# Seven products instead of eight for half of the first product in blocks 4 and 5, with their weight sums made in block 0, and 84 products of block 0 made as column halves

## The chip, the cores and the metric

The kernel runs on one core of one Trainium2 chip. A core has a matrix engine (TensorE, PE in the profile; its weight loads are the row PEld), a vector engine (VectorE, DVE), a scalar engine (ScalarE, ACT), GpSimd (POOL) and a queue processor that issues DMAs (SyncE, SP). Each engine works through its own instructions in order and waits for the others through semaphores. The metric is the device time of one execution in microseconds (us), lower is better; the kernel before takes 196.34 us, the median of three runs (196.23 to 196.53).

## The reference

Two parts, one behind the other. A recurrent attention without softmax over 4 batches, 8 heads, 768 steps, heads of 64:

```python
for t in range(S):
    state = gamma * state + outer(k[t], v[t])       # per batch and head, 64 x 64
    y[t] = scale * (q[t] @ state)
x = y, as 3072 tokens x 512
h = x @ w_in                                        # 512 -> 2048
g = h * tanh(softplus(h))                           # "mish"
out = g @ w_out                                     # 2048 -> 512, float32
```

The recurrence is computed in chunks of 128 steps (scores inside a chunk, a state between chunks), so nearly all of the work is matrix products: of the attention, the first product (x with W_in), and the second product (g with W_out).

## The kernel before, in words

The 24 chunks of 128 tokens are taken in 11 blocks. Block 0 has four chunks (512 tokens), blocks 1 to 10 have two (256 tokens). Operands are float16, sums are float32 in PSUM. For each block TensorE makes the first product, ScalarE applies mish, TensorE makes the second product, and between the products of the second one TensorE makes the attention of the block after (`retain`: past states, present scores, and with `later` also the scores and outer products of the block after that one). All instructions are written in the order that each engine runs them; there is no scheduler.

**The second product** of blocks 1 to 10 (`seven`, matrix products at L838) is cut into 2x2 parts and made with seven products of parts instead of eight (Winograd's form of Strassen's scheme). It needs sums of parts of g (`sums_a`, `sums_b`, `sums_c`: DVE, L699, L700, L704, L708, tile gsum) and of W_out (tmat, L683 to L686, made once in block 0). ScalarE copies partial results out (snap, L844), DVE adds them up into osb (`done`, L853 and L851), and SP stores osb (L226).

**The first product** has two forms.

- Plain (`g1`, L635), blocks 0 to 5: for each of 16 groups of 128 features, four matrix products over the 512 inputs; 64 instructions of 256 columns per block (block 0: of 512 columns), and eight mish (L643) of 128x512.
- Mixed (`mixed_in`), from block `MIX` = 6 on: half of the features (quarters 0 and 2 of W_in) by seven products of parts, 56 instructions of 128 columns (L745), the other half plain, 32 instructions of 256 columns (L765). The seven products need sums of W_in (`in_sums`, wsum, L716 to L719, made one operation at a time in blocks 4 and 5) and of x: `x_sums` (L732, four operations of 128x256 float16, two float16 tiles of SBUF in, one out), which DVE makes at the end of the second product of the block before. Results are put together from ScalarE copies (`kept`, L775) and DVE additions (`plus`, L780, tile hsum), then mish (L756).

In a mixed block the order on TensorE is: pa (8 products), a plain pair of groups (8), pf (8, needs the first x sum), a plain pair (8), pm, pa, pf (8 each), a plain pair (8), pa (8), a plain pair into the bank ph (8), pa (8). The bank ph is one that the scores of the block after have held: it comes free when DVE has made the mask product am (`mask_two`, L540) of them. The last pa products add onto a bank that DVE's third addition (h22) must have read. In the code:

```python
        h22 = plus(pa, m5)
        ...
        ph = atps.tile([P, 2, 2, 2 * C], FP32, name="h_ps", tag="at")[:, 0]
        plain(ph, 3 * n + 2)()
        mm(pa, a(1, 1), t[3])
```

On DVE, around the start of a mixed block, stand in this order: an osb sum, x sums 1 and 2, an osb sum, an osb copy, x sums 3 and 4, then the state of the block after (mid, sth, mid: L505 or L507, L516, L507), its mask am, and the three additions h11, h12, h22.

**GpSimd** casts and scales what the loads bring: for each chunk q (L414), k (L417) and v (L424), reading float32 and writing float16 in SBUF, 128x512 each. Where these casts stand is set by `cast_behind` (called in `seven`), which first copies one element of a gsum tile (tile summed, L1179) so that the casts come after that DVE sum, and by what `hooks` puts behind the attention: `next_two` up to block 4 (casts of two chunks), `next_one` from block 5 on. With `next_one` goes `second_of`, called at the start of blocks 6 and later: it first copies one element of the last x sum (L1161), then casts. Each cast pair is turned by a DMA transpose (L429) that SP issues.

**Block 0** loads the weights. Its first two feature groups are made by `open_in` (L620), the other 14 by `g1` (56 instructions of 512 columns), the second product by `g2_mm` without the seven-product scheme (64 instructions of 512 columns, L649). A table `plan` in `first_block` puts other work between its 32 steps: step 9, 12 and 16 cast quarters of W_out on DVE (L220), step 17 starts the W_out sums.

Of the kernel before, what the change touches and what calls it, by code (L numbers as in the profile page):

```python
# [16 lines left out]
def kernel(  # L17
# [9 lines left out]
    nc = tc.nc  # L27
    B, H, S, D = q.shape
    d_model, d_ff = moe_w_in.shape
    P = 128  # L30
# [8 lines left out]
    NFB = d_ff // P  # L39
# [79 lines left out]
    loaded, cast, qkts, ats, ams, states, mids, us, ys = {}, {}, {}, {}, {}, {}, {}, {}, {}  # L119
    xts, gts, wins, wouts, wtmps = {}, {}, {}, {}, {}  # L120
    gtiles, tmats, gsums = {}, [], []
    ONE, MIX = 3, 6
    nload, ncast = [0], [0]
    stores, weight_left, wsums = [], [], []

# [502 lines left out]
    def g1(blk, u):  # L628
        nt = BLOCKS[blk] * C
        per = TB // nt  # L630
        h_ps = g1_bank(blk, u)
        for j in range(per):
            s, f = divmod(u * per + j, FPS)
            for bp in range(NBP):
                nc.tensor.matmul(  # L635
                    h_ps[:, j], wins[s][f // 2][:, bp, f % 2 * P:(f % 2 + 1) * P], xts[blk][:, bp, :nt],
                    start=(bp == 0), stop=(bp == NBP - 1))
        room = NFB * TB // (2 * nt)
        at0, lies = divmod(u * per, room)
        if lies == 0:  # L640
            gtiles[blk, at0] = gp.tile([P, room, nt], FP16, name="g", tag="g", bufs=3)
        gt = gtiles[blk, at0][:, lies:lies + per]
        nc.scalar.activation(gt, h_ps, AF.Mish, scale=inv_boost3)  # L643
        for j in range(per):
            gts[blk, u * per + j] = gt[:, j]

    def g2_mm(o_ps, blk, t, fb, cols=slice(None)):
        s, f = divmod(fb, FPS)
        nc.tensor.matmul(  # L649
            o_ps, gts[blk, fb][:, t * P:(t + 1) * P], wouts[s][:, f, cols],  # L650
            start=(fb == 0), stop=(fb == NFB - 1))

    def out_rows(blk, t):
        if blk == 0:
# [306 lines left out]
    def first_block():  # L961
# [93 lines left out]
        def sum_weights(half, n):  # L1055
            if not weight_left:
                weight_left.extend(weight_sums(half))
            for _ in range(n):
                weight_left.pop(0)()

        plan = {
            9: [(cast_wout, 0)],
            12: [(cast_wout, 1)],
            16: [(cast_wout, 2), (load_more,), (cast_qk,)],
            17: [(sum_weights, 0, 3)],
            23: [(cast_wout, 3, True)],
# [91 lines left out]
    def second_of(blk):  # L1158
        g = first[blk] + 6
        if g < NCK:  # L1160
            nc.gpsimd.tensor_copy(summed, xts[blk + 1][:, 3, TB - 1:])  # L1161
            casts_qk(g + 1)
            turn_by_dma(g + 1)
            casts_v(g)
            casts_v(g + 1)
        store_due(NFB)
        load_to(g + 4)
# [8 lines left out]
    def cast_behind(blk, i):  # L1176
        g = first[blk] + (6 if blk == 1 else 8)
        if ncast[0] < min(g, NCK):
            nc.gpsimd.tensor_copy(summed, gsums[blk % 2][:, i, NFB // 2 - 1, P - 1:])  # L1179
            if blk == 1:  # L1180
                for n in range(g - 2, g):
                    casts_qk(n)
                for n in range(g - 2, g):
                    casts_v(n)
                ncast[0] = g
            elif blk + 1 >= MIX:
                cast_to(g - 2)
                casts_qk(g - 2)
                ncast[0] = g
            else:  # L1190
                cast_to(min(g, nload[0]))
# [5 lines left out]
    def plan_of(blk):  # L1197
        a = first[blk] + 4
        plan = {u: [] for u in (0, 1, 5)}
        if tight(blk):  # L1200
            plan[5] = [(get_ready, blk + 1)]
        elif blk < MIX:
            plan[0] = [(settle, blk + 1), (mask_two, blk + 1), (leave, blk + 1)]
        if blk == 1:
            plan[0] += [(load_to, a + 2)]
            plan[1] += [(begin_load, a + 2)]
        elif blk < ONE:
            plan[1] += [(next_chunk, a)]
        return plan

    first_block()
    for blk in range(1, len(BLOCKS)):
        last = blk + 1 == len(BLOCKS)
        plan = plan_of(blk)
        if blk >= MIX:
            second_of(blk - 1)
            mixed_in(blk, last)
        elif blk > ONE:
            weight_left.extend(in_sums(blk - ONE - 1))
        for u in range(NFB // 2 if blk < MIX else 0):  # L1220
            store_due(u)
            g1(blk, u)
            if u in ((6, 7) if tight(blk) else (5, 7)):
                sums_a(blk, u // 7)
            for fn, *args in plan.get(u, ()):
                fn(*args)
            if weight_left:
                weight_left.pop(0)()
        hooks = [[], [], []]
        if not last:  # L1230
            later = blk + 2 if ONE <= blk < len(BLOCKS) - 2 else None
            hooks = [[(retain, blk + 1, later)],
                     [(next_one, first[blk] + 6)] if blk + 1 >= MIX else
                     [(next_two, first[blk] + 6, tight(blk))] if blk >= ONE else
                     [(turn_load, first[blk] + 4)] if blk == 1 else
                     [(next_chunk, first[blk] + 5), (turn_load, first[blk] + 6)],
                     [(finish, blk + 1)] if later is None else []]
        if tight(blk):
            hooks[2].append((leave, blk + 1))
        seven(blk, [(mask_two, blk + 1)] if tight(blk) else [], hooks, last)  # L1240
# [31 lines left out]
```

## Time and profile before

| what | value |
|---|---|
| median of three runs | 196.34 us (196.23 to 196.53) |
| the profiled execution's own time | 196.27 us |
| its span, first to last instruction | 194.5 us |
| granted TensorE clock | 0.998 of full |
| busy: PE, DVE, ACT, POOL | 189.6, 128.7, 99.5, 73.3 us |
| block 4, plain: first product, whole block | 6.99, 14.45 us |
| block 5, plain: first product, whole block | 6.99, 14.44 us |
| block 6, mixed: first product, whole block | 6.69, 14.21 us |
| block 7, mixed: first product, whole block | 6.69, 14.04 us |

The rows on blocks come from the chain of work that ended last, by the start of each block's first product (93.75, 108.20, 122.64, 136.85 and 150.89 us). In a row of a timeline the first number is the start in us from the begin of the span, the second the duration, then engine, line of the kernel, operation and tiles; in square brackets is the idle time before it and what ended it. The work outside the span (196.27 less 194.5) is 1.8 us.

### The profile page before, as it was taken

How to read it: one execution, taken by the hardware profiler on the slowest of the kernel's cores; microseconds unless marked ns; L12 is line 12 of the kernel's file. 1: busy time of each engine (PE TensorE's matmuls, PEld its weight loads, DVE VectorE, ACT ScalarE, POOL GpSimd, SP SyncE). 2: the span in 40 equal slices, each digit the busy share in tenths (PEclk: the TensorE clock that was granted, in tenths of full speed). 3: DMA queues.
4: the chain of work that ended last, by engine and by line, in shares of the span. 5: the costliest groups of instructions: out<-in, count | busy, mean ns of one | idle time of the engine just before them, and what ended most of it. 6: DMA issues, size and time to landing. Idle time of an engine off the chain costs nothing.

```text
span 194.5 us, 6886 instructions
## 1 busy us (share of the span) xinstructions
PE 189.6 (97%) x2996; PEld 154.0 (79%) x2996; DVE 128.7 (66%) x248; ACT 99.5 (51%) x183; POOL 73.3 (38%) x96
## 2 busy tenths in 40 slices
PE   7998999999999999999999999999999999999994
PEld 7756444454888888888888888998998998988983
DVE  0796535889767378467884864965885885876462
ACT  3375764243553552554364364584574663763750
POOL 5262000549508746562826605525625700000000
PEclk9999999999999999999999999999999999999999
DMA  5999999999999999999999999889996250300202
GB/s 172 304 309 349 368 386 366 293 302 202 202 260 248 157 233 225 214 175 216 261 207 227 278 192 287 103 225 245 77 223 123 50 150 5 111 0 20 95 27 81
DMA packets 84285, 38.75 MB, mean 199 GB/s; under 512 B 57760, under 2 KB 78880, under 8 KB 84256
## 3 DMA queue, kind: packets, MB, share of 16 engines
q1 hardware_dynamic: 84112, 38.28, 84.7%
q8 instruction: 23, 0.38, 0.9%
q10 hardware_dynamic: 144, 0.05, 0.1%
q14 instruction: 6, 0.05, 0.1%
HBM read 27.31 MB, written 6.29 MB: 173 GB/s over the span
## 4 chain that ended last, share of the span: by engine, by line
PE 93%; DMA 3%; ACT 1%; DVE 1%; issue 1%; SPq 0%
PE o_ps L838 32%; PE h_ps L635 24%; PE h_ps L765 9%; PE h_ps L745 8%; PE o_ps L649 7%; PE y_ps L551 3%; DMA qfirst<-in_q_dram 3%; PE u_ps L479 1%; PE at L472 1%; PE t_ps L247 1%; PE y_ps L373 1%; PE h_ps L620 1%; PE at L443 1%; PE at L327 1%; DVE qk L259 1%
## 5 line engine op out<-in xcount | busy, mean ns | idle before, releaser
L635 PE MATMUL h_ps<-xt,win 128*128 128x256 f16 (+1 forms) x376 | 48.5, 289 | 0.0
L635 PEld LDWEIGHTS <-win 128*128 128x128 f16 x376 | 36.5, 98 | 10.4 <-issue 0.2
L643 ACT ACTIVATE g<-h_ps 128x512 f16<-128x512 f32 x54 | 32.2, 597 | 23.7 <-PE h_ps L635 23.7
L838 PEld LDWEIGHTS <-gsum 128*128 128x128 f16 x320 | 30.3, 98 | 3.8
L838 PE MATMUL o_ps<-tmat,gsum 128*128 128x256 f16 x240 | 29.8, 273 | 0.0
L838 PEld LDWEIGHTS <-g 128*128 128x128 f16 x248 | 23.4, 98 | 2.7
L853 DVE TENSOR_TENSOR osb<-o_ps,snap 128x256 f32<-128x256 f32 (+1 forms) x33 | 13.8, 418 | 14.0 <-PE o_ps L838 8.9
L844 ACT COPY snap<-o_ps 128x256 f32<-128x256 f32 (+1 forms) x33 | 12.2, 370 | 20.7 <-PE o_ps L838 20.7
L414 POOL TENSOR_TENSOR qk<-qf,qvs 128x512 f16<-128x512 f32 x18 | 19.2, 1065 | 4.8 <-DMA qf<-in_q_dram 4.7
L765 PE MATMUL h_ps<-xt,win 128*128 128x256 f16 x160 | 20.7, 273 | 0.0
L424 POOL TENSOR_TENSOR v<-vf,qvs 128x512 f16<-128x512 f32 x18 | 19.7, 1101 | 1.2 <-DMA vf<-in_v_dram 1.0
L417 POOL TENSOR_TENSOR qk<-kf,qvs 128x512 f16<-128x512 f32 x18 | 19.1, 1060 | 2.7 <-DMA kf<-in_k_dram 2.6
L838 PE MATMUL o_ps<-wout,g 128*128 128x256 f16 x160 | 19.1, 273 | 0.0
L1179 POOL COPY summed<-gsum 128x1 f16<-128x1 f16 x7 | 3.0, 432 | 37.2 <-DVE gsum L704 29.8
L765 PEld LDWEIGHTS <-win 128*128 128x128 f16 x160 | 14.8, 98 | 1.4
L756 ACT ACTIVATE g<-h_ps 128x512 f16<-128x512 f32 x25 | 14.2, 588 | 2.4 <-PE h_ps L765 2.4
L600 ACT CAST xt<-y_ps 128x512 f16<-128x512 f32 x15 | 10.2, 734 | 10.2 <-PE y_ps L551 10.2
L649 PE MATMUL o_ps<-wout,g 128*128 128x512 f16 x64 | 15.0, 380 | 0.0
L780 DVE TENSOR_TENSOR hsum<-h_ps,hsum 128x512 f32<-128x512 f32 x15 | 10.4, 692 | 6.1 <-PE h_ps L745 4.4
L775 ACT COPY hsum<-h_ps 128x512 f32<-128x512 f32 x15 | 8.8, 585 | 10.5 <-PE h_ps L745 10.5
L699 DVE TENSOR_TENSOR gsum<-g 128x512 f16<-128x512 f16 x20 | 9.2, 459 | 5.2 <-ACT g L643 3.1
L507 DVE TENSOR_TENSOR mid<-u_ps,sth 128x256 f16<-128x256 f32 x15 | 6.3, 422 | 8.5 <-PE u_ps L479 8.2
(99 smaller groups left out, 277.7 us busy)
## 6 DMA issues: line engine op xcount, KB each, us to landing
kf<-in_k_dram SPq DMA_DIRECT2D x24, 256.0 KB, 5.3
vf<-in_v_dram SPq DMA_DIRECT2D x24, 256.0 KB, 5.5
out_dram<-osb SPq DMA_DIRECT2D x22, 256.0 KB, 3.5
qf<-in_q_dram SPq DMA_DIRECT2D x20, 256.0 KB, 4.3
wi<-in_moe_w_in_dram SPq DMA_DIRECT2D x6, 512.0 KB, 8.7
wt<-in_moe_w_out_dram SPq DMA_DIRECT2D x3, 1024.0 KB, 10.3
qfirst<-in_q_dram SPq DMA_DIRECT2D x2, 512.0 KB, 4.6
wi<-in_moe_w_in_dram SPq DMA_DIRECT2D x1, 1024.0 KB, 10.0
```

The lines of the kernel that those rows point to most:

```text
L414: nc.gpsimd.tensor_tensor(in_place(q16.rearrange("p (w x) d -> p w x d", x=2)), by_head(qf), scale_by_head(qs_two[:, heads]), op=ALU.mult)
L417: nc.gpsimd.tensor_tensor(k16.rearrange("p (y w) d -> p w y d", y=2), kf.rearrange("p (w y) d -> p w y d", y=2), boosts.rearrange("p (w y) ...
L424: nc.gpsimd.tensor_tensor(cast[g][2], loaded.pop(g)[2], vs[g % 2].unsqueeze(2).broadcast_to((P, H, D)), op=ALU.mult)
L635: nc.tensor.matmul(h_ps[:, j], wins[s][f // 2][:, bp, f % 2 * P:(f % 2 + 1) * P], xts[blk][:, bp, :nt], start=(bp == 0), stop=(bp == NBP - 1))
L643: nc.scalar.activation(gt, h_ps, AF.Mish, scale=inv_boost3)
L649: nc.tensor.matmul(o_ps, gts[blk, fb][:, t * P:(t + 1) * P], wouts[s][:, f, cols], start=(fb == 0), stop=(fb == NFB - 1))
L745: nc.tensor.matmul(o_ps[:, f], w(f // 2, k)[:, f % 2 * P:(f % 2 + 1) * P], x[:, k], start=begin and f == 0 and k == 0, stop=k == 1, skip_g ...
L756: nc.scalar.activation(to, src, AF.Mish, scale=inv_boost3)
L765: nc.tensor.matmul(h_ps[:, f], wins[w][h // 2][:, k, h % 2 * P:(h % 2 + 1) * P], xts[blk][:, k, :2 * C], start=k == 0, stop=k == NBP - 1)
L838: nc.tensor.matmul(o_ps[:, cols], x(f), w(f)[:, cols], start=first and z == 0, stop=z == n - 1, skip_group_check=True)
L844: nc.scalar.copy(x, o_ps[:, cols])
L853: nc.vector.tensor_tensor(dst, o_ps[:, cols], plus, op=ALU.add)
```

## The change

Three things are changed.

- `MIX` goes from 6 to 4: blocks 4 and 5 take the mixed form. What the old number also decided about casts and loads (`next_one`, `second_of`, the form of `cast_behind`) now goes by a new number `BACK`, which stays at 6: GpSimd's and SP's instructions stand in the same order as before.
- The sums of W_in (two sets of four operations) are made in block 0, at steps 10 and 13, instead of in blocks 4 and 5.
- In block 0 the last 24 instructions of the first product (feature groups 10 to 15) and 60 of the second (all but the first feature group) are each made as two instructions of 256 columns with the same weights.

```diff
-    ONE, MIX = 3, 6
+    ONE, MIX, BACK = 3, 4, 6
...
             for bp in range(NBP):
-                nc.tensor.matmul(
-                    h_ps[:, j], wins[s][f // 2][:, bp, f % 2 * P:(f % 2 + 1) * P], xts[blk][:, bp, :nt],
-                    start=(bp == 0), stop=(bp == NBP - 1))
+                for i, at in enumerate(in_halves(nt) if blk == 0 and u >= NFB - 6 else [slice(nt)]):
+                    nc.tensor.matmul(
+                        h_ps[:, j, at], wins[s][f // 2][:, bp, f % 2 * P:(f % 2 + 1) * P],
+                        xts[blk][:, bp, at], start=(bp == 0 and i == 0), stop=(bp == NBP - 1),
+                        skip_group_check=True)
...
+    def in_halves(n):
+        return slice(n // 2), slice(n // 2, n)
+
+    def g2_mm(o_ps, blk, t, fb):
         s, f = divmod(fb, FPS)
-        nc.tensor.matmul(
-            o_ps, gts[blk, fb][:, t * P:(t + 1) * P], wouts[s][:, f, cols],
-            start=(fb == 0), stop=(fb == NFB - 1))
+        for cols in in_halves(d_model) if fb > 0 else [slice(d_model)]:
+            nc.tensor.matmul(
+                o_ps[:, cols], gts[blk, fb][:, t * P:(t + 1) * P], wouts[s][:, f, cols],
+                start=(fb == 0), stop=(fb == NFB - 1), skip_group_check=True)
...
+        def sum_win(j):
+            for fn in in_sums(j):
+                fn()
+
         plan = {
             9: [(cast_wout, 0)],
+            10: [(sum_win, 0)],
             12: [(cast_wout, 1)],
+            13: [(sum_win, 1)],
             16: [(cast_wout, 2), (load_more,), (cast_qk,)],
...
-            elif blk + 1 >= MIX:
+            elif blk + 1 >= BACK:
                 cast_to(g - 2)
...
+        if blk >= BACK:
+            second_of(blk - 1)
         if blk >= MIX:
-            second_of(blk - 1)
+            store_due(NFB)
             mixed_in(blk, last)
-        elif blk > ONE:
-            weight_left.extend(in_sums(blk - ONE - 1))
...
-                     [(next_one, first[blk] + 6)] if blk + 1 >= MIX else
+                     [(next_one, first[blk] + 6)] if blk + 1 >= BACK else
```

## The prediction

> **What bounds the kernel now.** I read the page's busy table first, then the chain of waits, then the DVE, GpSimd and ScalarE timelines around the starts of blocks 4, 5 and 6. The busy table:
>
> ```profile
> PE 189.6 (97%) x2996; PEld 154.0 (79%) x2996; DVE 128.7 (66%) x248; ACT 99.5 (51%) x183; POOL 73.3 (38%) x96
> ```
>
> TensorE is never idle for long, so a change counts by what it does to TensorE's own time, or by a wait that it puts into it. The chain (start, length, what) gives the prices:
>
> ```profile
> 19.50 12.09 PE h_ps L635 x56
> 31.59 7.77 PE o_ps L649 x36
> 93.75 6.99 PE h_ps L635 x64
> 108.20 6.99 PE h_ps L635 x64
> ...
> 122.64 0.45 PE h_ps L745 x8
> 123.09 0.87 PE h_ps L765 x8
> ...
> 128.81 0.52 PE h_ps L745 x8
> 129.33 3.49 PE o_ps L838 x32
> ```
>
> A plain first product takes 6.99 us, a mixed one 129.33 - 122.64 = 6.69 us, with only one gap of 0.07 us in it (0.52 against 0.45 in its last group). Products of 512 columns come at 12.09/56 = 215.9 ns, of 256 at 6.99/64 = 109.2 ns.
>
> A mixed block leans on DVE. How DVE does beside GpSimd is in the timelines (start, duration, engine, line):
>
> ```profile
> 35.88 2.56 POOL L297 TENSOR_TENSOR qk<-qf,qvs 128x512 f16<-128x512 f32 x2 [18.05 <-DMA qf<-in_q_dram]
> 36.01 1.53 DVE L683 TENSOR_TENSOR tmat<-wout 128x1024 f16<-128x1024 f16 x1
> 37.57 1.42 DVE L684 TENSOR_TENSOR tmat<-wout,tmat 128x1024 f16<-128x1024 f16 x1
> 38.91 0.68 DVE L685 TENSOR_TENSOR tmat<-wout,wout 128x1024 f16<-128x1024 f16 x1
> ...
> 85.52 1.23 POOL L424 TENSOR_TENSOR v<-vf,qvs 128x512 f16<-128x512 f32 x1
> 85.88 1.15 DVE L700 TENSOR_TENSOR gsum<-gsum,g 128x512 f16<-128x512 f16 x1
> 91.38 1.04 POOL L414 TENSOR_TENSOR qk<-qf,qvs 128x512 f16<-128x512 f32 x1
> 92.38 1.04 POOL L417 TENSOR_TENSOR qk<-kf,qvs 128x512 f16<-128x512 f32 x1
> 93.38 1.04 POOL L424 TENSOR_TENSOR v<-vf,qvs 128x512 f16<-128x512 f32 x1
> 95.14 1.04 POOL L414 TENSOR_TENSOR qk<-qf,qvs 128x512 f16<-128x512 f32 x1 [0.73 <-DMA qf<-in_q_dram]
> 123.02 0.48 DVE L732 TENSOR_TENSOR xt<-xt 128x256 f16<-128x256 f16 x2
> 126.83 0.69 DVE L780 TENSOR_TENSOR hsum<-h_ps,hsum 128x512 f32<-128x512 f32 x1 [0.30 <-ACT hsum L775]
> 127.98 0.69 DVE L780 TENSOR_TENSOR hsum<-h_ps,hsum 128x512 f32<-128x512 f32 x1 [0.46 <-PE h_ps L745]
> ```
>
> L700 takes 0.42 us when alone; with a GpSimd cast under way it takes 1.15 and ends (87.03) 0.28 us after the cast (86.75). L716 at 97.39 (1.26 us, else 0.42), L699 at 70.64 (1.20) and L520 at 78.94 (0.96) end 0.29, 0.28 and 0.28 us after a cast too. All read two SBUF tiles. The first rows show who goes next: a DVE sum waits for one cast, the next cast waits for that sum (two casts in 2.56 us, not 2.08), and the second sum waits for that cast. They alternate. Additions with one operand in PSUM show nothing of it (all 32 osb sums at 0.42).
>
> A trap for mixed blocks: the twenty x sums (L732) of blocks 6 to 10 run in 281 to 293 ns each, but in those blocks GpSimd is idle then. At the starts of blocks 4 and 5 it is not.
>
> **The change part by part.**
>
> *First product of blocks 4 and 5, TensorE's own time:* 2 x (6.69 - 6.99) = -0.60 us.
>
> *Halves in block 0:* 84 products become 168: 84 x (2 x 109.2 - 215.9) = 84 x 2.5 = +0.21 us, in full, as TensorE is dense there. The added weight loads (98 ns mean) hide behind 256 columns in every L635 and L838 row, at 109 ns a product. Bounds: 0, and 84 x 98 = 8.2 us if no load were hidden; the nearest rows are at 0.21.
>
> *W_in sums in block 0:* eight L716 to L719 rows, one set in 1.55 us without a cast beside it (111.75 to 113.30). DVE idles 1.49 and 1.55 us before the second and third W_out cast (32.09, 34.86; it waits for DMA), and the sets stand just there; GpSimd is idle (18.05 us before 35.88). The casts come at most 0.1 us late; TensorE uses quarter 1 at 31.59 + 16 x 0.216 = 35.0 (cast done 33.3) and quarter 2 at 38.5 (done 36.1). Cost 0, covered by 1.7 us at least. The sums leave blocks 4 and 5: DVE is not the bound there, gain 0.
>
> *ScalarE, SP, GpSimd:* a mixed block keeps ScalarE busy for 8.5 of 14 us, where it was 7.2; by itself no wait. GpSimd's and SP's orders are unchanged. SP's store of block 3 waits for the osb copy, about 1.2 us later than now (below); behind it stand three loads (kf landing 5.3 us after issue, cast near 104) and two transposes (4.2 us, needed with the scores at 105, themselves later by then): 0.
>
> *x sums at the start of block 4, beside casts that run from 91.38:* times are this trace's.
> - x1 can start at 92.47 (its input, ACT's xt, ends at 92.45). The cast of k holds until 93.42; x1 ends 0.15 later (0.28 less the 0.13 by which it is shorter than L700), at 93.57. The waiting cast of v goes next, to 94.5; x2 ends at 94.65.
> - Two osb operations (0.34 apart) bring DVE to 95.25. The next q cast starts at 95.14: x3 ends at 96.33, the k cast at 97.3, x4 at 97.45.
> - From x4's end to the mask's end is 2.38 us in block 6 (123.50 to 125.88): the mask ends at 99.83. TensorE wants the bank ph 5.30 us into the block (127.94 - 122.64), at 99.05: it waits 0.8 us.
> - h11, h12, h22 follow at 0.6 us each, h22 ends at 101.65. TensorE's last group would start at 100.75: it waits 0.95 us. In block 6 this costs nothing because DVE idles 0.30 + 0.46 us before h12 and h22.
> - Six mish queue up behind h11 on ScalarE, 0.55 us apart, the last done at 103.8; the second product reads it at 103.45: 0.35 us.
> Sum 2.1, less the 0.07 gap that 6.69 holds: +2.05 us.
>
> *Block 5*, with the casts of 104.21 to 110.25 in one row: x1 waits until 107.25, x2 for the next cast (ends 108.5), osb operations to 109.2, x3 ends 109.5, x4 110.6, mask 112.98 (wanted at 113.5: no wait), h22 114.8 against 114.35: 0.45, and the same mish queue 0.35: +0.8 us.
>
> *Bounds of the collisions.* Below: if x3 and x4 of block 4 slip in before a q cast that DMA lets in 0.6 us later, block 4 keeps only its mish queue, 0.4: together 1.2. Above: eight sums, each behind a whole cast of 1.04 us, less the 0.9 us of DVE slack per block: 2 x (4.2 - 0.9 + 0.35) = 7.3; but x1 and x3 meet casts already under way, so I take the sum of the row's own phases, 2.85.
>
> A rule bears on this. The Trainium skill, Advanced Engine Details and Errata, VectorE Performance Modes, says that GpSimd blocks two-port VectorE modes; by it a sum of two tensors, which is in none of them, would go free, and the change would be worth -0.4. The skill's SBUF — State Buffer, Who interferes with whom, says that a VectorE instruction with two SBUF inputs contends with a GpSimd one that reads SBUF, and that the second fully blocks. The 1.15 us of L700 side with the skill's SBUF page.
>
> Sum: -0.60 + 0.21 + 2.05 + 0.8 = +2.46. The profiled execution took 196.27 (span 194.5 and 1.77 around it; the median of the runs is 196.34, 0.07 more): 198.7 us.
>
> **The rivals.**
> - *No collision* (other side). The x sums take 0.29 us each, as all twenty do now; then DVE's slack of 0.9 us per block is untouched and the time is 196.27 - 0.39 = 195.9. For it: the twenty rows. Against it: four sum rows that end 0.28 us after a cast, and casts that cover 92.38 to 94.42 and all of 104.21 to 110.25. It decides if the sums delay DVE's third addition by under 0.9 us in each block. By the Trainium skill's Advanced Engine Details and Errata it would be this.
> - *Half the waits.* Two sums in a row keep the port, or the q cast at 95.14 comes late: block 4 pays 0.4, block 5 0.8: -0.39 + 1.2: 197.1. For it: x3 and that cast are 0.1 us apart, and the cast waits for a DMA. Against: the alternation at 36 to 38 us.
> - *The lag feeds on.* DVE's lag delays sums_b, and so the casts that wait for it, and the transposes for the scores of later blocks: 1 us more, 199.7 or above. Against: from block 6 on GpSimd idles 3 us before the x sums.
> - *The halves cost weight loads.* Up to 8 us; no row of 256 columns shows it.
>
> **How the numbers follow.** Forecast (both blocks collide, 197.5 to 199.5) 0.65; half the waits 0.14; no collision 0.15; above 199.7 0.06. The predicted time is 198.7. The range 195.9 to 199.7 reaches down to the no-collision case, since forecast and half the waits alone would leave out 0.21. A run can tell about 0.2% (0.4 us). No collision sits at that bound (-0.2%) and is split: faster 0.08, same 0.07, slower 0.85.
>
> **What would show it.** In the changed profile: L649 and block 0's L635 at 109 ns per half and block 0 0.2 us longer; W_in sums at 30.5 to 34.8 us in 0.42 us each; x sums before blocks 4 and 5 of about 1 us where GpSimd casts, and 0.29 from block 6 on; gaps in TensorE before the last plain pair (ph) and the last seven-product group of block 4, before the latter alone in block 5, with DVE's am and hsum as releasers; first products of about 8.4 and 7.1 us, and 0.35 us more in each second product. Wrong would make it: x sums of 0.29 us beside casts, or TensorE without gaps there.

## The result

The changed kernel takes 197.12 us (median of six runs, 196.96 to 197.28) where the kernel before takes 196.30 (six runs on the same chip, 196.23 to 196.53). The ratio is 1.0040, with a 95% interval of 1.0027 to 1.0053: slower by 0.8 us. Twelve later runs on another chip gave 1.0048 (1.0022 to 1.0074). The direction was forecast; the forecast of +2.46 us was three times too large.

TensorE's busy time fell by 0.3 us although it has 132 products more. The busy table of the profile after, and the row of the queue that carries code, which will matter below:

```profile
PE 189.3 (97%) x3128; PEld 161.6 (83%) x3128; DVE 134.8 (69%) x262; ACT 101.9 (52%) x189; POOL 73.4 (38%) x96
...
q8 instruction: 24, 0.39, 0.9%
```

The chain of the profile after (start, length, what), at the places that the prediction showed of before:

```profile
19.49 12.15 PE h_ps L636 x80
31.63 7.85 PE o_ps L655 x68
...
115.34 4.68 DMA qkt<-qk
120.02 0.04 issue
120.06 0.38 PE at L472 x24
...
123.29 0.45 PE h_ps L751 x8
123.74 0.87 PE h_ps L771 x8
...
129.47 0.52 PE h_ps L751 x8
129.98 3.49 PE o_ps L844 x32
```

The halves cost 0.06 and 0.08 us in the two long rows, and block 1 starts at 49.05 us where it started at 48.86. A mixed first product is 129.98 - 123.29 = 6.69 us, as before. New in this part of the chain is the DMA: the scores in the turn into block 6 wait for a transpose. In the kernel before the same scores have no such wait:

```profile
119.30 0.46 PE L472 MATMUL at<-qkt 64*64 64x64 f16 x30
```

The sums that were said to collide, in the timelines of the profile after (start, duration, engine, line, and in brackets the idle time before):

```profile
92.65 2.15 DVE L738 TENSOR_TENSOR xt<-xt 128x256 f16<-128x256 f16 x2
95.38 0.48 DVE L738 TENSOR_TENSOR xt<-xt 128x256 f16<-128x256 f16 x2
95.72 1.04 POOL L414 TENSOR_TENSOR qk<-qf,qvs 128x512 f16<-128x512 f32 x1 [1.08 <-DMA qf<-in_q_dram]
107.18 1.53 DVE L738 TENSOR_TENSOR xt<-xt 128x256 f16<-128x256 f16 x2
109.29 0.66 DVE L738 TENSOR_TENSOR xt<-xt 128x256 f16<-128x256 f16 x2
110.63 1.04 POOL L424 TENSOR_TENSOR v<-vf,qvs 128x512 f16<-128x512 f32 x1 [1.02 <-DMA vf<-in_v_dram]
120.06 0.38 PE L472 MATMUL at<-qkt 64*64 64x64 f16 x24 [0.56 <-DMA qkt<-qk]
```

The first pair of block 4 collided as forecast (2.15 us, ending at 94.80; forecast 94.65). The second pair did not (0.48 us), because the load that GpSimd's next cast needs landed late and the cast began at 95.72, not at 95.14. The load was put on its queue at 89.22 us (88.88 before) and took 6.3 us to land (6.1), so it was late before any sum had collided. In block 5 a late load, of v, kept the second pair nearly free too (0.66 us).

To compare kernels I use three stretches of TensorE's timeline, cut at the attention products y_ps (L551) of each turn between two blocks: S4 from the last of them in the turn into block 4 to the first in the turn into block 5, S5 the same for block 5, and S6 from the first y_ps product of the turn into block 6 to that of the turn into block 7. All are taken from start to start, "the last" being the last group of them. S6 holds the scores (L472) that waited. In the kernel before they start at 90.69, 105.14 and 118.61 us.

| profile of | S4 | turn into 5 | S5 | S6 |
|---|---|---|---|---|
| before | 13.47 | 0.97 | 13.47 | 14.15 |
| after | 13.56 | 0.97 | 13.17 | 14.84 |

Without any wait a stretch with a mixed block would be 13.47 - 0.30 = 13.17. So block 4 paid 0.39 for its collisions (0.10 before pf, the first group that needs an x sum, and 0.29 at the start of the second product, whose weight loads wait for mish), block 5 nothing, and S6 lost 0.69 to the transpose. With the halves: 0.17 - 0.60 + 0.39 + 0.69 = +0.65 of the 0.69 us by which the two profiled executions differ (196.96 and 196.27).

### The profile page after: what moved, and what is told of

Same layout as the page of the kernel before. It is cut to its first block, busy times and chain, and to the rows that moved or that the text cites. A ratio compares the mean times of both kernels' runs of the same rounds, so it can differ in the third digit from the quotient of the medians.

```text
span 195.2 us, 7178 instructions
## 1 busy us (share of the span) xinstructions
PE 189.3 (97%) x3128; PEld 161.6 (83%) x3128; DVE 134.8 (69%) x262; ACT 101.9 (52%) x189; POOL 73.4 (38%) x96
## 4 chain that ended last, share of the span: by engine, by line
PE 68%; DMA 14%; SPq 7%; POOL 4%; issue 2%; DVE 2%; ACT 1%; POOLq 0%
PE o_ps L844 21%; PE h_ps L636 14%; PE h_ps L771 9%; PE h_ps L751 8%; PE o_ps L655 7%; DMA vf<-in_v_dram 6%; SPq L429 3%; SPq L162 3%; DMA qf<-in_q_dram 3%; DMA qfirst<-in_q_dram 3%; DMA qkt<-qk 2%; POOL v L424 2%; PE y_ps L551 2%; PE t_ps L247 1%; POOL qk L414 1%
## 5 line engine op out<-in xcount | busy, mean ns | idle before, releaser
L636 PE MATMUL h_ps<-xt,win 128*128 128x256 f16 (+1 forms) x272 | 34.3, 285 | 0.0
L636 PEld LDWEIGHTS <-win 128*128 128x128 f16 x272 | 26.3, 98 | 6.6
L645 ACT ACTIVATE g<-h_ps 128x512 f16<-128x512 f32 x38 | 22.7, 597 | 15.5 <-PE h_ps L636 15.5
L771 PE MATMUL h_ps<-xt,win 128*128 128x256 f16 x224 | 29.0, 273 | 0.0
L771 PEld LDWEIGHTS <-win 128*128 128x128 f16 x224 | 20.7, 98 | 1.9
L762 ACT ACTIVATE g<-h_ps 128x512 f16<-128x512 f32 x35 | 19.9, 589 | 3.4 <-PE h_ps L771 3.4
L424 POOL TENSOR_TENSOR v<-vf,qvs 128x512 f16<-128x512 f32 x18 | 19.5, 1092 | 1.7 <-DMA vf<-in_v_dram 1.5
L781 ACT COPY hsum<-h_ps 128x512 f32<-128x512 f32 x21 | 12.3, 586 | 14.9 <-PE h_ps L751 14.9
L786 DVE TENSOR_TENSOR hsum<-h_ps,hsum 128x512 f32<-128x512 f32 x21 | 14.2, 690 | 6.4 <-PE h_ps L751 4.6
L751 PE MATMUL h_ps<-xt,wsum 128*128 128x128 f16 x224 | 15.9, 219 | 0.0
L655 PE MATMUL o_ps<-wout,g 128*128 128x256 f16 (+1 forms) x124 | 15.2, 276 | 0.0
L751 PEld LDWEIGHTS <-wsum 128*128 128x128 f16 x224 | 14.0, 98 | 0.4
```

The lines of the kernel that those rows point to most:

```text
L424: nc.gpsimd.tensor_tensor(cast[g][2], loaded.pop(g)[2], vs[g % 2].unsqueeze(2).broadcast_to((P, H, D)), op=ALU.mult)
L636: nc.tensor.matmul(h_ps[:, j, at], wins[s][f // 2][:, bp, f % 2 * P:(f % 2 + 1) * P], xts[blk][:, bp, at], start=(bp == 0 and i == 0), sto ...
L655: nc.tensor.matmul(o_ps[:, cols], gts[blk, fb][:, t * P:(t + 1) * P], wouts[s][:, f, cols], start=(fb == 0), stop=(fb == NFB - 1), skip_gr ...
L751: nc.tensor.matmul(o_ps[:, f], w(f // 2, k)[:, f % 2 * P:(f % 2 + 1) * P], x[:, k], start=begin and f == 0 and k == 0, stop=k == 1, skip_g ...
L762: nc.scalar.activation(to, src, AF.Mish, scale=inv_boost3)
L771: nc.tensor.matmul(h_ps[:, f], wins[w][h // 2][:, k, h % 2 * P:(h % 2 + 1) * P], xts[blk][:, k, :2 * C], start=k == 0, stop=k == NBP - 1)
```

## The experiments

Two theories at first. *A*: the loss is the collisions, and the late transpose is their consequence. *B*: DMA is full in blocks 2 to 5 (in block 4 of the kernel before its share is 1.05 of the engines' time) and sets when the transposes land; what TensorE wins before, it waits for at L472. A third, *F*, came from the first run.

**Without the halves.**

```diff
-                for i, at in enumerate(in_halves(nt) if blk == 0 and u >= NFB - 6 else [slice(nt)]):
+                for i, at in enumerate([slice(nt)]):
...
-        for cols in in_halves(d_model) if fb > 0 else [slice(d_model)]:
+        for cols in [slice(d_model)]:
```

> The changed kernel without the 84 column halves in block 0, all else kept. Theory A (the 0.8 us are: halves 0.2, collisions of VectorE with GpSimd in blocks 4 and 5 about 0.5, a wait for a DMA transpose about 0.6, less 0.6 for the smaller products): the stretch up to block 1 gets back to 48.9 us from 49.05, all else moves with it, 196.9 us, about 0.2 less than the changed kernel. Theory B (the DMA queue sets the pace from block 2 to the scores of block 7, and whatever TensorE gains or loses before is made up in the wait at L472): block 1 starts 0.2 earlier too, but the wait at L472 in block 5 grows by the same 0.2, and the time stays 197.1 us.

Measured: 200.9 us (six runs, 199.46 to 202.36), ratio to before 1.0228 (1.0188 to 1.0267). Neither theory had this: the halves, which cost 0.2 us, save 3.8. TensorE's timeline has waits that end with nothing that the profile shows ("issue"):

```profile
95.67 0.44 PE L751 MATMUL h_ps<-xt,wsum 128*128 128x128 f16 x5 [0.33 <-issue]
110.56 0.71 PE L771 MATMUL h_ps<-xt,win 128*128 128x256 f16 x5 [1.30 <-issue]
124.62 0.44 PE L751 MATMUL h_ps<-xt,win 128*128 128x128 f16 x5 [0.35 <-issue]
138.41 0.70 PE L844 MATMUL o_ps<-wout,gsum 128*128 128x256 f16 x5 [1.01 <-issue]
153.23 0.71 PE L844 MATMUL o_ps<-tmat,gsum 128*128 128x256 f16 x5 [1.50 <-issue]
```

They fall at different lines, which speaks against an operand as the cause. But counted through the trace from 0 (3044 products, each with its weight load) they stand before products 1375, 1631, 1887, 2143 and 2399: 256 products apart, and all 95 beyond a multiple of 128. 128 products with their weight loads are 256 instructions, and the queue named "instruction" carries 23 packets of 16 KB. One of them ends 1.39 to 1.64 us before each of the five waits ends. The DMA view of this kernel for 135.9 to 137.1 us shows one of them, between the others' traffic:

```profile
q1 hardware_dynamic: 1102, 0.28, 123.7%
q8 instruction: 1, 0.02, 5.7%
```

So theory F: TensorE's code comes in pieces of 256 instructions. The packet for the next piece starts 1.1 to 3.5 us after the current one was begun (in these five cases), takes 1.0 us and is usable 1.4 to 1.6 us later. A piece that is worked off sooner than that ends in a wait. The attention in the turn between two blocks is 120 or 128 products of 64x64 in 1.1 to 1.3 us, nearly a whole piece, so a piece that has most of a turn in it is short: without halves, pieces begun at 104.68, 134.82 and 149.46 us held 4.6, 2.6 and 2.3 us of work. In the kernel before, by its own trace, no piece from block 1 on holds under 4.98 us. (It has one such wait at its start, 0.40 us at 15.42 us, before product 223, which is 95 beyond 128 too.)

The change adds 48 products in blocks 4 and 5 (24 each), and that shifts all later pieces by 48, to where the turn fits into one. With the 84 of the halves the shift is 132, that is one whole piece and 4: nearly the old cut. That is what the halves do. The Trainium skill, Advanced Engine Details and Errata, ISA Cache, gives the size (a line of 16 KB, 256 instructions, two lines); the trace agrees with the size: 6000 instructions of the kernel before and 23 packets. The Trainium skill's Runtime: NRT & Kernel Launch, Instruction fetch mechanics, calls the crossing "mostly hidden"; here it is not, with 4.5 us of waits.

**The halves alone.**

```diff
-    ONE, MIX, BACK = 3, 4, 6
+    ONE, MIX, BACK = 3, 6, 6
```

> The other part alone: the column halves and the W_in sums in block 0 are kept, blocks 4 and 5 make eight products for all of the first product as before. Theory A: the kernel before plus the 0.2 us of the halves, 196.5 us; no x sums in blocks 4 and 5, so no collision there, and GpSimd's six casts of that stretch as in the kernel before. Theory B: the transpose comes as late as the DMA queue lets it, and blocks 4 and 5 are 0.6 us longer on TensorE, so the wait at L472 is at or near 0 and the time 196.3 to 196.5 us. The two differ here only in the wait: under A there is none, as in the kernel before; under B it is what is left of 0.6 after TensorE's longer blocks.

Measured: 197.43 us (twelve runs, 196.78 to 198.5), 1.0056 (1.0036 to 1.0075); profiled at 196.78. Above both expectations. S4 and S5 are those of before (13.47), there are no x sums in blocks 4 and 5, and still:

```profile
119.86 0.38 PE L472 MATMUL at<-qkt 64*64 64x64 f16 x24 [0.44 <-DMA qkt<-qk]
```

So the late transpose needs neither a collision nor shorter blocks: against theory A. The rest of the runs go up to 198.5, which this profile doesn't explain. Shifting the kernel before by 84 products, its trace gives pieces down to 3.0 us, so waits for code in some runs are possible, but not shown.

**A forced collision in block 4.**

```diff
+            elif blk == 3:
+                cast_to(g - 1)
+                fill()
+                cast_to(min(g, nload[0]))
```

`fill` is one GpSimd multiplication of 128x512 into a tile that nothing reads.

> The changed kernel with one more GpSimd operation of 128x512 (about 1 us, its result is not used) between the casts of chunk 14 and those of chunk 15, that is, where GpSimd stood idle while the second pair of x sums of block 4 ran. Theory A: the second pair collides as the first does, x3 and x4 end 1.0 to 1.5 us later, the mask and the sums behind it too, and products of block 4 wait for them: 0.4 to 1.0 us more in block 4, and q casts 0.6 to 1.0 later with the loads behind them, so 197.6 to 198.4 us. Theory B: block 4 gets longer by the collision but the wait at L472 shrinks by it, unless the casts' delay reaches the transposes: 197.1 to 197.4 us.

Measured: 197.51 us (ten runs, 196.94 to 198.13), 1.0054 (1.0037 to 1.0072); profiled at 197.20. The second pair of block 4 now takes 1.51 us, S4 is 13.87 (0.31 more than in the profile after) and S5 13.97. S6 is 14.14, with no wait. The waits for collisions rose by 0.31 + 0.80, the wait for the transpose fell by 0.70. The time lies between the two theories' ranges: A left out that exchange. The transpose landed at 119.9 us, and TensorE came to its scores later than that.

**The x sums taken off VectorE.**

```diff
+            if blk < BACK:
+                nc.scalar.copy(to, a)
+                continue
```

> The changed kernel with the x sums of blocks 4 and 5 made as ScalarE copies of their first operand: the subtraction or addition is left out there, so the second operand isn't in them. VectorE then has none of the eight operations in these blocks and cannot collide in them, GpSimd's and the queue's orders stay. Theory A: block 4 loses its 0.39 us of small waits, block 5 its share of about 0.1, casts run on time and the wait at L472 goes with them; 196.1 to 196.4 us. Theory B: blocks 4 and 5 lose their small waits, but the wait for the transpose takes it up, 0.6 to 1.0 us at L472, and the time stays 196.7 to 197.1 us.

The kernel leaves out the subtractions of these sums. Measured: 196.78 us (twelve runs, 196.08 to 198.59), 1.0031 (1.0004 to 1.0058); profiled at 197.28. S4 is 13.17 and S5 13.15: without collisions the products give their 0.30 and 0.32. But S6 is 15.15:

```profile
120.03 0.38 PE L472 MATMUL at<-qkt 64*64 64x64 f16 x24 [0.87 <-DMA qkt<-qk]
```

The transpose lands at 120.0 us here, in the kernel after and (119.86) with the halves alone. TensorE comes sooner and waits longer, as theory B says. That holds for the profiled run: five of the twelve runs took 196.08 to 196.44 us, which is about theory A's range, so they can hardly have paid all of such a wait.

**The same with four stores less.**

```diff
-                stores.append((1 + i, out_rows(blk, i), osb[i]))
+                if blk not in (1, 2):
+                    stores.append((1 + i, out_rows(blk, i), osb[i]))
```

> The run with ScalarE copies in place of the x sums of blocks 4 and 5 (the subtraction left out there), and beside it the stores of the outputs of blocks 1 and 2 left out: four transfers of 256 KB less on the queue, so those rows of the output are not written. Theory B (full DMA engines set when the transpose for the turn into block 6 lands, near 120.0 us whatever TensorE does): with some 4 us of transfers less it lands earlier, the wait of 0.87 us at L472 goes, and the gain of the smaller products is seen for once, 196.3 + 0.2 - 0.6 = 195.9 us or a little more. Theory A (the transpose is late since VectorE holds up GpSimd's casts): there is no such hold-up in either of the two runs, so the stores make no difference and the wait stays, 196.7 us.

Measured: S4 13.17, S5 13.17, S6 14.14, no wait at L472: with 1 MB less to move, the transpose is in time (it lands at 118.2 us). The last attention products (turn into the last block) start at 174.60 us, in the kernel before at 175.05: 0.45 sooner, the 0.60 - 0.17 of the sum. The whole time does not show it: 196.78 us (twelve runs, 196.51 to 197.07), 1.0009 (0.9995 to 1.0022). VectorE's last output operation begins 0.46 us sooner than in the kernel before (191.21 and 191.67), but 0.36 us more pass after it within the span, and 2.13 us instead of 1.77 outside. Both kernels with ScalarE copies have the longer time outside, and both with four stores less the longer end within the span (19.8 us from the start of the last attention products, 19.4 to 19.5 in all other profiles); why, I haven't found. So the gain of 0.45 is shown up to the last block, and not in the time of the kernel.

**48 products more in the kernel before.** 48 of block 0's second product as halves, nothing else.

```diff
+        for at in [slice(0, d_model // 2), slice(d_model // 2, d_model)] if fb > 3 else [slice(d_model)]:
+            nc.tensor.matmul(
+                o_ps[:, at], gts[blk, fb][:, t * P:(t + 1) * P], wouts[s][:, f, at],
```

> The kernel before, with 48 products of block 0's second product made as two column halves and nothing else. TensorE then has 3044 products, as many as the changed kernel without its halves, and from block 3 on each product has the same number in the stream as there. Theory F (TensorE's code comes in pieces of 16 KB, 256 instructions, which are 128 products with their weight loads; the next but one is asked for when a piece is begun and takes 3.5 to 6 us; where a piece holds the 48 small products of a block's turn and little else it runs out in 2.3 to 4.6 us and TensorE waits): the waits of 0.3 to 1.5 us once per block come as in the run without halves, at products 95 mod 128, some 4.5 us in all, and the time is 196.3 + 0.1 + 4.5, 200.9 us. Theory S (the seven products of blocks 4 and 5 wait by themselves for their operands there): none of these waits, 196.4 us.

Measured: 204.12 us (four runs, 203.96 to 204.6), 1.0373 (1.0329 to 1.0418). The waits stand at the same five products, 95 beyond a multiple of 128, in a kernel whose first products in blocks 4 and 5 are plain:

```profile
91.78 0.23 PE L551 MATMUL y_ps<-am,v 64*64 64x64 f16 x5 [0.53 <-issue]
108.16 0.71 PE L839 MATMUL o_ps<-wout,gsum 128*128 128x256 f16 x5 [0.40 <-issue]
124.80 0.44 PE L746 MATMUL h_ps<-xt,win 128*128 128x128 f16 x5 [0.45 <-issue]
139.64 1.21 PE L839 MATMUL o_ps<-wout,gsum 128*128 128x256 f16 x5 [2.06 <-issue]
155.43 0.71 PE L839 MATMUL o_ps<-tmat,gsum 128*128 128x256 f16 x5 [0.81 <-issue]
```

Theory F is shown, and the seven products have no part in it. The time is above F's 200.9, in part because the clock fell after the wait of 2.06 us, and 2.5 us instead of 1.8 pass outside the span. The windows of this kernel (length, busy time and count of PE, PEld, DVE, ACT and POOL, the granted clock, DMA share, GB/s):

```profile
130.00:137.00 7.00, 7.00 (x186) 6.17 (x184) 4.09 (x9) 4.17 (x10) 2.51 (x3) 1.00 1.14 262
137.00:144.00 7.00, 4.95 (x35) 3.87 (x33) 2.76 (x9) 1.27 (x3) 0.45 (x2) 0.76 0.73 71
```

The 0.76 is a mean: the clock was at 0.50 from 139.69 to 143.10 us. The next 13 products of 256 columns took 2.91 us instead of 1.58, and eight of 128 columns 0.77 instead of 0.45.

**The count made up elsewhere.** No halves; 120 products of 64x64 for 36 of the 46 that keep TensorE busy at the start.

```diff
-        spin(46, 1)
+        spin(10, 1)
+        for _ in range(120):
+            nc.tensor.matmul(
...
+                start=True, stop=True)
```

> The changed kernel without the column halves; instead, 36 of the 46 products of 128 columns that keep TensorE busy while the first loads are under way are replaced by 120 of 64x64, so the stream has 84 more products again, all in time in which TensorE has nothing else to do. Theory F: pieces of code begin at the same products as in the changed kernel, no wait for code, and block 1 starts 0.2 us earlier: 196.9 us where the changed kernel has 197.1, less if the wait at L472 doesn't take the 0.2. Theory S: the halves matter where they are, in block 0; without them 200.9 us as in the run without halves.

Measured: 206.32 us (six runs, 205.62 to 206.97), 1.0486 (1.0445 to 1.0527). Nearly all of the loss is at the start: the attention of the turn into block 2 begins 8.4 us later than in the profile after, of 8.7 us by which the profiled times differ.

```profile
2.54 6.61 PE L980 MATMUL at<-ident 64*64 64x64 f16 x120
...
23.20 0.61 PE L373 MATMUL y_ps<-am,v 64*64 64x128 f16 x15 [3.32 <-issue]
```

The small products take 55 ns each, so the first transposes begin at 9.08 us, not 6.19; the work from there to the first scores (L327) takes 4.63 us, where it took 3.13; then the code for a piece comes 3.32 us late, while the weights are being loaded, and the clock is at 0.50 for 3.4 us after it. From block 1 on there is no wait for code, S4 is 13.74, S5 13.97, S6 14.14. So the count is what matters and not block 0, as F says; the expected gain failed, as this piece at the start held only 3.1 us of work and its packet began 3.8 us after the piece.

**One order on SP changed.** In block 4 the second transpose ahead of the loads.

```diff
-                     [(next_two, first[blk] + 6, tight(blk))] if blk >= ONE else
+                     [(next_two, first[blk] + 6, True)] if blk >= ONE else
```

> The changed kernel with one order changed: in block 4 the two DMA transposes of the next chunks stand ahead of the last three loads on SP, as they do in block 3, so the transpose that the scores in block 5 wait for is issued three loads (1.7 us) earlier. If the wait of 0.56 us at L472 is a matter of the place in the queue, it is gone: 196.5 us. If the DMA engines are full and every transfer is put off alike, the transpose lands as late, or the loads behind it come late and another wait of 0.5 us comes in block 5 or 6: 197.0 to 197.3 us.

Measured: 197.12 us (twelve runs, 196.38 to 197.9), 1.0020 (0.9997 to 1.0043), on the chip on which the changed kernel itself gave 197.68. S6 is 14.14, so that wait is gone, but the turn into block 5 takes 1.58 instead of 0.97 us. S4 is 13.17: a cast waited 1.88 us for its load and left the second pair alone.

```profile
96.12 1.04 POOL L424 TENSOR_TENSOR v<-vf,qvs 128x512 f16<-128x512 f32 x1 [1.88 <-DMA vf<-in_v_dram]
105.98 0.38 PE L472 MATMUL at<-qkt 64*64 64x64 f16 x24 [0.47 <-DMA qkt<-qk]
```

The wait at 105.98 is before the changed order acts (at 110.73 us), so it is scatter of the landing and no effect of the edit. The run decides little, except that the same kernel can lose at another turn.

**The changed kernel once more.**

> The changed kernel as it is, on the chip of this series, so that the others are held against it there: 197.0 to 197.3 us with the wait at L472 between 0 and 0.9 us, if that wait depends on when transfers land; no wait for code, since 132 more products than before are 4 more than a piece of 128.

Measured: 197.68 us (twelve runs, 196.91 to 198.94), 1.0048 (1.0022 to 1.0074); profiled at 197.67. No wait at L472. Instead both blocks pay for collisions, block 4 twice as much as in the first profile:

```profile
92.80 1.41 DVE L738 TENSOR_TENSOR xt<-xt 128x256 f16<-128x256 f16 x2
94.80 1.66 DVE L738 TENSOR_TENSOR xt<-xt 128x256 f16<-128x256 f16 x2
100.69 0.61 PE L751 MATMUL h_ps<-xt,win 128*128 128x128 f16 x8 [0.45 <-DVE hsum L786]
107.79 1.52 DVE L738 TENSOR_TENSOR xt<-xt 128x256 f16<-128x256 f16 x2
109.90 1.51 DVE L738 TENSOR_TENSOR xt<-xt 128x256 f16<-128x256 f16 x2
115.64 0.61 PE L751 MATMUL h_ps<-xt,win 128*128 128x128 f16 x8 [0.40 <-DVE hsum L786]
```

S4 is 14.01, S5 13.98, S6 14.14: 0.84 + 0.81 + 0 where the first profile had 0.39 + 0 + 0.69. The expectation named the wait and not the collisions.

**The changed kernel with four stores less** (the edit of the stores above).

> The changed kernel without the stores of the outputs of blocks 1 and 2 (those rows of the output are not written), so four transfers of 256 KB fewer. If the loads' landing decides which of the two losses is paid: loads land in time, GpSimd's casts run without gaps, both pairs of x sums collide in both blocks, blocks 4 and 5 take 13.9 to 14.0 us each instead of 13.17, and there is no wait at L472; 196.3 + 0.2 - 0.6 + 1.7, 197.5 us: freeing the queue makes it no faster. If the collisions are as in the first profile of the changed kernel whatever the loads do (0.39 and 0.02 us): 196.3 us.

Measured: 198.02 us (six runs, 197.56 to 198.41), 1.0080 (1.0058 to 1.0101). Less traffic did not help; by the ratios, 1.0080 here and 1.0040 and 1.0048 for the changed kernel on two other chips, it was slower. All casts of blocks 4 and 5 run with next to no gap, and all pairs collide:

```profile
92.63 2.14 DVE L738 TENSOR_TENSOR xt<-xt 128x256 f16<-128x256 f16 x2
95.35 1.51 DVE L738 TENSOR_TENSOR xt<-xt 128x256 f16<-128x256 f16 x2
101.09 0.61 PE L751 MATMUL h_ps<-xt,win 128*128 128x128 f16 x8 [0.76 <-DVE hsum L786]
108.19 1.53 DVE L738 TENSOR_TENSOR xt<-xt 128x256 f16<-128x256 f16 x2
110.31 1.51 DVE L738 TENSOR_TENSOR xt<-xt 128x256 f16<-128x256 f16 x2
116.05 0.61 PE L751 MATMUL h_ps<-xt,win 128*128 128x128 f16 x8 [0.42 <-DVE hsum L786]
```

S4 is 14.59, more than the 13.9 to 14.0 expected, S5 13.98, S6 14.14: 196.27 + 0.17 - 0.60 + 1.42 + 0.81 = 198.07. The profiled run took 198.41; the rest is the longer end seen above. The landing of the loads decides which loss is paid.

**Wide products at the start, no halves.** A shift of 11 instead of 48 or 4.

```diff
-        spin(46, 1)
+        spin(46)
...
-        spin(14, 2)
+        spin(14)
```

> The changed kernel without the column halves, and the 53 narrow products that keep TensorE busy at the start made as 16 products of 512 columns, over as many columns in all: the stream is 37 products shorter from the start. Against the kernel before, the products from block 6 on stand 11 later in it, where they stand 48 later without this and 4 later with the halves. Theory F: with 11 the shortest piece of 128 products takes 4.0 us by the trace of the kernel before, where 48 gives 1.8, so there is no wait for code, or one of at most 0.5 us in a block, and with block 0 back to its length the time is 196.9 us (with the collisions or the wait at L472 as in the changed kernel). Theory S: without halves 200.9 us again.

Measured: 201.68 us (six runs, 199.41 to 202.57), 1.0235 (1.0183 to 1.0287). Again the loss is at the start, with a wait of 2.75 us for code at 18.52 us and a clock of 0.50 for 3.4 us behind it. From block 1 on there is none, with S4 13.75, S5 13.97, S6 14.14. F's numbers for the shift held, its time did not.

**The casts of blocks 4 and 5 behind the x sums,** as in blocks 6 and later.

```diff
-    ONE, MIX, BACK = 3, 4, 6
+    ONE, MIX, BACK = 3, 4, 4
```

> The changed kernel with blocks 4 and 5 ordered as blocks 6 and later: GpSimd's casts of each block stand behind the x sums (BACK = 4), so the two cannot collide, and the transposes' and loads' order on SP is that of the later blocks. Theory A: blocks 4 and 5 take 13.17 us each where the kernel before has 13.47, and the time is 196.3 + 0.2 - 0.6, 195.9 us, if the casts, begun 1 to 3 us later, still feed the transposes in time. Theory B: the transposes are late by what the casts are, 1 to 3 us, and waits at L472 in blocks 4 and 5 cost more than the 1.1 us won: 197 to 199 us.

Measured: 195.84 us (twelve runs, 195.76 to 197.55) beside 196.48 of the kernel before, 0.9978 (0.9959 to 0.9998). On another chip:

> The gated version once more, beside the kernel before on another chip, for its usual run: blocks 4 and 5 of 13.17 us each; where no transpose comes late, 195.84 us, 0.43 under the kernel before (0.60 from the smaller products less 0.17 for the halves); where one does, 0.9 to 1.2 us more. If its gain was that chip's alone: no lower than the kernel before here.

Measured: 196.09 us (twelve runs, 195.76 to 197.0) beside 196.36, 0.9989 (0.9974 to 1.0004). The second profile, 195.83 us, has S4 13.17, S5 13.17, S6 14.16 and no wait; 196.27 + 0.17 - 0.60 is 195.84. The sums there (block 4, then block 5):

```profile
92.63 1.41 DVE L738 TENSOR_TENSOR xt<-xt 128x256 f16<-128x256 f16 x2
94.62 0.48 DVE L738 TENSOR_TENSOR xt<-xt 128x256 f16<-128x256 f16 x2
106.77 0.62 DVE L738 TENSOR_TENSOR xt<-xt 128x256 f16<-128x256 f16 x2
108.43 0.48 DVE L738 TENSOR_TENSOR xt<-xt 128x256 f16<-128x256 f16 x2
```

The first pair of block 4 still meets one cast, which VectorE's slack covers. The first profile, 197.55 us, shows what other runs pay: the turn into block 5 takes 2.14 us, with 0.90 us of it a wait for a transpose at L472, and block 1 started late besides. This is the version that beats the changed kernel clearly, and the kernel before by 0.3 to 0.6 us of median, at the edge of what can be measured: the interval of the second comparison takes in 1.

**The gated version with the transposes ahead of the loads.**

```diff
     def next_one(g):
+        if g < first[5] + 6:
+            turn_by_dma(g)
         load_to(g + 3)
-        if g < NCK:
+        if first[5] + 6 <= g < NCK:
             turn_by_dma(g)
```

> The gated version with one more order changed: in blocks 3 and 4 the transpose that the next block's scores need is put on SP ahead of the three loads that stood before it. In the profiled run of the gated version that transpose was late (0.9 us at L472 at 106.5 us), while most of its runs took 195.84 us. Theory A and B together (collisions gone by the gate; what is left is when the transposes land): the runs with the late transpose become fewer and the median stays at 195.8 us, blocks 4 and 5 13.17 us each with no wait at L472. If instead the loads put behind the transpose come late for the casts of the next block, a wait of 0.5 to 1 us comes one turn later, and the time is 196.4 to 197 us.

Measured: 196.48 us (twelve runs, 195.83 to 197.86), 0.9992 (0.9961 to 1.0022). A miss: the profile has a wait of 1.06 us at L472 at the same turn as the gated version. The second of the two transposes is issued at 101.56 us, still behind the loads.

## Why the prediction was right or wrong

- **Smaller products, -0.60: right.** S4 and S5 are 13.15 to 13.18 us, 0.30 below before, wherever no collision delays TensorE.
- **Halves, +0.21: right as a cost (0.17), blind to the rest.** The prediction weighed only weight loads against them. It never asked what 48 more products do to where TensorE's code is cut; without the halves the change costs 4.6 us. In the sum this cancels, so it didn't spoil the number.
- **W_in sums in block 0, 0: right.** They stand at 30.54 to 32.16 and 33.25 to 34.80 us, as forecast, and the casts of W_out that follow begin at 32.11 and 34.88 (32.09 and 34.86 before).
- **Collisions: the mechanism right.** Sums of two SBUF tiles wait until the cast under way has ended: pairs of 1.41 to 2.15 us where they meet casts, and 0.48 to 0.62 alone. So the Trainium skill's SBUF — State Buffer, Who interferes with whom, describes this chip here, and the narrower rule that the prediction took from the Trainium skill's Advanced Engine Details and Errata, VectorE Performance Modes, by which they would go free, does not.
- **The term of block 4, +2.05: the step that failed.** It was 1.66 us too large, where the whole forecast was 1.64 too large (+2.46 for +0.82); the errors of the two terms below, 0.8 too large and 0.69 too small, nearly cancel. The prediction took the cast phases of the trace of before as fixed and x3 as behind the q cast at 95.14. That cast waits for a DMA; in the changed kernel's profile it came at 95.72, and the term measured 0.39: the waits before ph and for h22 did not come, and the mish queue was all but 0.10 of it. The prediction's lower bound named just this. With the casts on time (four stores less) it measured 1.42: the first pair ended as forecast, but the second at 96.86, not 97.45, and the wait before ph was 0.18 (a plain pair starts at 99.30 where the group before it would let it start at 99.12), not 0.8. The q cast, with no wait for its load, began at 94.58 there.
- **The term of block 5, +0.8: right for casts without gaps** (0.80 or 0.81 in five profiles, S5 of 13.97 or 13.98 less 13.17), and 0 in the first profile of the change, where a load came late.
- **SP and its transposes, 0: wrong.** The prediction looked at the store of block 3 and the scores at 105 us, but not at those at 119.25. Their transpose was issued at 114.07 in the kernel before and took 4.5 us to land, at 118.6: a margin of 0.7 us. In the first profile of the change it was issued at 115.34, landed 4.7 us later, and cost 0.69.
- **The rivals.** "Half the waits" gave nearly the measured time (197.1), and its reason for block 4, a late q cast, is what happened; but it charged block 5 0.8 where the profile shows 0, and the transpose, which it had at 0, makes up the difference: its number was luck. "No collision" is what the ScalarE copies showed to be worth little by itself, with 1.0 us of wait in S6, and what the gated version got in its good runs: 195.84, where that rival said 195.9.

What remains open is why the transpose lands later than in the profile of the kernel before (118.6 us). In all five profiles with the halves, the old order and all stores it lands at 119.6 to 120.0 us, with collisions and without: the changed kernel twice, the halves alone, the forced collision, the ScalarE copies. With the halves alone it is issued 0.33 us later (114.40) and takes 5.4 us; in the profile after it is issued 1.27 us later and takes 4.7. There SP's issues are 0.15, 0.34 and 0.69 us behind those of before at 81.5, 87.1 and 92.3 us, and 1.2 at 102.0; 0.2 of it is the halves, the rest I can't assign. Scatter isn't ruled out: the kernel before has one profile only, and single runs of it on the later chips took up to 198.63 us.

## What to carry to other kernels

Where DMA is full, as here, the phase of an engine that waits for loads is not a fixed number (one q cast began at 94.58, 95.22 and 95.72 us in three profiles): cost a collision by both phases, and ask which loss takes the place of one that goes away, since here collisions and the wait for the transpose paid each other's bill. Put the two engines in order (a cast behind the sum) instead of hoping for the phase. And where an instruction stream is long, count what an edit adds before a stretch of many short instructions, modulo the size of a code piece: here 48 products too many cost 3.8 us, and 7.6 us in the kernel before.

## What was unexpected of the hardware

- Code for TensorE is a transfer like others and can be late: 23 or 24 packets of 16 KB in a run of 195 us, each usable, where TensorE waited for it, 1.3 to 1.7 us after it has ended, and waits of 0.3 to 2.06 us from block 3 on and up to 3.32 us at the start, where a piece of 256 instructions is worked off before the next packet is there.
- A wait of 2.06 us was followed by a granted clock of 0.50 for 3.4 us, which made it cost some 1.65 us more (2.91 - 1.58 + 0.77 - 0.45). The waits of 2.75 and 3.32 us at the start have the same behind them; those of 1.50 us and less have not.
- Less traffic did not make a kernel faster: the changed kernel without four of its stores takes 198.02 us, where it took 197.12 and 197.68 with them, on other chips.
